# A fused adaLN transformer block on one core, its 2121 operations in another order from a new table

## The chip, the core and the metric

The kernel runs on one core of one Trainium2 chip. The core has five instruction streams that run side by side and wait for one another through semaphores: TensorE (PE, matmuls; the profile shows its weight loads apart as PEld), VectorE (DVE), ScalarE (ACT), GpSimd (POOL) and SyncE (SP, which here only issues transfers). The metric is the device time of one execution in microseconds (us); lower is better.

## The reference

The input x has 2048 rows of 640 values in bf16. A conditioning vector c gives six modulation rows, and then one transformer block is computed:

```python
mod = (silu(c) @ w_mod).reshape(1, 6, 1, -1)
sa, ca, ga, sb, cb, gb = (mod[:, i] for i in range(6))
h = layernorm(x) * (1 + ca) + sa
x = x + ga * attention(h, A_wqkv, A_wo)
h = layernorm(x) * (1 + cb) + sb
x = x + gb * (sigmoid(h @ B_w_gate) * (h @ B_w_up)) @ B_w_down
```

The attention has 32 heads of 20 values and a sliding window: row i sees the rows i - 255 to i. The hidden width of the gated part is 1536.

## The kernel before

The rows are cut into eight chunks of 256, numbered a = 0 to 7, each of two blocks of 128. For every chunk the kernel does the same steps:

- `ln1`, with `ln_stats` (L776 to L796): statistics on VectorE, the power -1/2 on GpSimd (L781, L783), the normalised block x. For the first three chunks TensorE transposes it (`pe_transposes`), and the evacuation from PSUM applies scale and shift (L858; for chunk 0 copies L839 and then modulations L846 and L847). For the other chunks SyncE transposes it by a transfer (L803) and `modulate` (L811, L812) applies scale and shift to the five parts of hT, each on VectorE, ScalarE or GpSimd.
- `qkv`: projections with wqkv (TensorE, 480 columns a matmul, 320 for chunk 0) and their evacuation (L893 on ScalarE, L894 on VectorE); Q and K are then transposed, by TensorE for chunks 0 and 1 and by SyncE's transfers for the others.
- `attention`: in two halves (q = 0, 1) of 16 heads. A half has five score groups (three for chunk 0), four of one kind and one edge group at the window's borders. All score groups write the one PSUM tile S of four banks. ScalarE takes the exponential of S into E (L1015), GpSimd zeroes what lies outside the window (L1040), and a burst of matmuls E V (L669) writes two of the four other PSUM tiles, M. The burst of one half is issued together with the second score group of the next half. `norm` on VectorE transposes, divides and transposes back (L1082, L1087, L1089, L1091), and SyncE stores the result in eight pieces in `doc` and loads it transposed as oT.
- `outproj`: output projection with wo, the first residual sum (L1164), the second layernorm, transposed by SyncE into h2T and modulated (L811, L812).
- `mlp`: twelve pairs of 128 hidden columns; matmuls with wg and wu, tanh on ScalarE (L1209), the gated product on VectorE into hh (L1211), the matmuls with wd, the second residual sum (L1230) and the store.

At the start the modulation rows are computed by matmuls of silubc (silu of c, spread) with w_mod, which lies for that time in the room of wd, wu and hh. The first two rows end as mA, needed for the first modulation. The gate rows ga and gb are spread over all partitions by a small store and a load into gbc (`gate`, `gatebc` in `mod_rows`), and multiplied into wo (L1253, five operations) and later into wd (L1192, twelve operations, VectorE or GpSimd). There is one gbc: the second load waits till the five scalings of wo have read the first. At the very start TensorE runs matmuls on zeros (L649, L660), whose result is not used.

Nothing of the order is left to the hardware or a compiler. The program makes 2121 operations in a fixed numbering, and a table `PRIO` holds one number for each. The scheduler sorts by it, and the number modulo 5 names the engine:

```python
o.prio = PRIO[self.seq] if PRIO else prio
...
for o in sorted(self.ops, key=lambda x: x.prio):
    ...
    e = ENGS[o.prio % 5]
```

ENGS is TensorE, ScalarE, VectorE, GpSimd, SyncE in that order. The walk through the sorted operations also hands out the buffers: a tile takes the slot that comes free first. Each engine's stream is then its operations in that order, with a wait on a semaphore wherever an operation depends on another engine or on a buffer's last reader (`emit`). Each engine runs its stream strictly in order, so an operation that waits holds all that stand behind it. SyncE's stream is all transfers and transposes but a few that ScalarE issues.

Of the kernel before, what the change touches and what calls it, by code (L numbers as in the profile page):

```python
# [336 lines left out]
def c_pe(n):  # L337
# [5 lines left out]
    23, 28, 258, 8, 43, 33, 958, 18, 1448, 38, 3, 507, 513, 72, 67, 48, 53, 58, 76, 84, 101, 99, 144, 149, 154, 159,  # L343
    164, 344, 169, 334, 329, 174, 584, 734, 739, 754, 604, 759, 749, 764, 594, 120, 177, 181, 192, 197, 62, 105,
    110, 115, 130, 135, 13, 125, 200, 205, 210, 215, 220, 225, 230, 345, 370, 352, 599, 2054, 1659, 1649, 729, 744,
    92, 87, 187, 237, 242, 247, 253, 263, 272, 267, 280, 275, 290, 300, 305, 286, 317, 296, 322, 311, 376, 357, 386,
    367, 362, 412, 422, 391, 417, 396, 380, 400, 406, 620, 655, 672, 515, 521, 820, 827, 465, 470, 476, 530, 535,
    541, 495, 501, 665, 677, 480, 485, 491, 565, 570, 576, 545, 551, 630, 652, 525, 555, 561, 625, 660, 681, 685,
    691, 930, 977, 765, 770, 792, 915, 920, 927, 805, 810, 816, 830, 835, 841, 437, 432, 442, 427, 447, 452, 458,
    463, 642, 647, 890, 845, 775, 900, 710, 897, 852, 797, 907, 787, 980, 985, 996, 1150, 1165, 1171, 1095, 1101,  # L350
    1375, 1382, 1195, 1250, 1257, 1262, 1210, 1296, 1385, 1392, 990, 1105, 1111, 1080, 1085, 1092, 1365, 1371, 1300,
    1351, 940, 945, 951, 971, 1155, 1161, 1190, 1231, 1215, 1220, 1226, 1280, 1285, 1292, 1330, 1337, 1344, 1619,
    1347, 1502, 2249, 1434, 2959, 1669, 1622, 1917, 1932, 2107, 2137, 1395, 1497, 1664, 2754, 1627, 1847, 339, 589,
    1022, 637, 1037, 802, 782, 912, 1043, 1048, 1053, 1058, 1237, 1485, 1410, 1455, 1435, 1305, 1492, 1421, 1462,
    1442, 1317, 1570, 1575, 1581, 1515, 1520, 1527, 1844, 1585, 1590, 1632, 1751, 1839, 1905, 1965, 2041, 2020,
    2030, 2037, 2059, 2070, 2080, 2086, 2142, 2094, 1820, 1830, 1922, 1970, 2075, 2152, 719, 724, 1007, 1002, 1017,
    1012, 937, 1027, 1033, 1063, 1068, 1203, 1242, 1209, 1249, 1453, 1548, 1536, 1543, 1471, 605, 611, 616, 695,
    706, 701, 855, 961, 881, 871, 861, 968, 888, 878, 868, 1115, 1127, 1122, 1137, 1142, 1147, 1736, 1716, 1726,
    1416, 1944, 1070, 1076, 1131, 1175, 1181, 1186, 1265, 1321, 1401, 1356, 1271, 1328, 1408, 1363, 1278, 1505,
    1597, 1512, 1602, 1612, 1772, 1896, 1891, 1886, 1881, 2049, 2310, 2315, 2322, 2155, 2160, 2327, 2205, 2210,  # L360
    2227, 2395, 2400, 2432, 2337, 2332, 2507, 2437, 2502, 2512, 2518, 2523, 2527, 2537, 2534, 2544, 2717, 2756,
    2777, 2772, 2767, 2739, 2734, 2969, 3074, 3022, 3312, 3327, 3027, 3032, 3037, 3317, 3502, 3507, 3322, 3413,
    3418, 2865, 2870, 2875, 2890, 2895, 2760, 2845, 2880, 2885, 2905, 2901, 2912, 3045, 3050, 3075, 3080, 3085,
    2915, 2920, 3055, 3060, 3065, 3091, 3097, 3110, 3115, 3170, 3175, 3180, 3100, 3105, 3185, 3195, 3200, 3191,
    3232, 3205, 3210, 3215, 3220, 3225, 3240, 3245, 3250, 3265, 3270, 3236, 3277, 3280, 3285, 3290, 3295, 3330,
    3300, 3375, 3380, 3385, 3390, 3336, 3422, 3430, 3435, 3445, 3450, 3470, 3440, 3575, 3580, 3585, 3590, 3476,
    3597, 3640, 3645, 3655, 3727, 3650, 3730, 3780, 3817, 3859, 3740, 3745, 3750, 3827, 3900, 3905, 3910, 3917,
    4476, 1700, 1705, 1862, 1710, 1800, 1902, 1914, 1690, 1695, 1746, 1782, 2189, 2390, 2405, 2412, 2145, 2300,
    2307, 2429, 2250, 2260, 2267, 2616, 2749, 1865, 1875, 1937, 1825, 1975, 1992, 1429, 1314, 1607, 1637, 1787,
    1767, 1777, 1792, 1798, 1853, 2008, 2178, 1963, 2128, 2184, 2134, 2367, 2371, 2386, 2381, 2376, 1465, 1481,  # L370
    1476, 1530, 1556, 1566, 1670, 1731, 1676, 1721, 1741, 1805, 1816, 1811, 1870, 1946, 2001, 2025, 2061, 2066,
    1553, 1763, 1758, 1563, 1688, 1683, 1928, 1858, 1953, 1958, 2013, 2018, 2095, 2101, 2231, 2202, 2217, 2222,
    2592, 2597, 2984, 2964, 2999, 2989, 3129, 2255, 2286, 2271, 2341, 2281, 2345, 2351, 2356, 2440, 2456, 2451,
    2465, 2485, 2496, 2460, 2580, 2587, 3399, 2695, 2700, 2817, 2951, 3409, 2620, 2625, 2631, 2445, 2490, 2562,
    3404, 2665, 2670, 2787, 2792, 4199, 2640, 2655, 2662, 2705, 2710, 2841, 1654, 1644, 1997, 1987, 2122, 1982,
    2112, 2117, 2168, 2173, 2193, 2243, 2603, 2608, 2424, 2744, 3346, 3261, 3306, 3041, 3011, 2565, 2576, 2571,
    2238, 2298, 2293, 2198, 2473, 2278, 2363, 2483, 2478, 2548, 2553, 2558, 2635, 2676, 2686, 2652, 2647, 2782,
    2812, 2822, 2974, 2994, 2979, 3004, 3124, 3545, 3550, 3557, 3455, 3540, 3562, 3530, 3535, 3677, 3610, 3615,
    3682, 3572, 3567, 3672, 3687, 3692, 3697, 3703, 3708, 3867, 3712, 3929, 3719, 4213, 4208, 4081, 4132, 4232,
    4220, 4280, 4285, 4290, 4325, 4215, 4310, 4315, 4320, 4335, 4331, 4357, 4345, 4350, 4370, 4375, 4380, 4340,  # L380
    4390, 4395, 4400, 4405, 4386, 4412, 4420, 4425, 4430, 4435, 4440, 4415, 4540, 4545, 4550, 4555, 4511, 4582,
    4560, 4565, 4570, 4585, 4605, 4590, 4595, 4610, 4615, 4620, 4696, 4702, 4705, 4710, 4715, 4725, 4755, 4720,
    4730, 4735, 4800, 4805, 4761, 4812, 4815, 4820, 4825, 4830, 4840, 4835, 4845, 4855, 4860, 4865, 4851, 4872,
    4900, 4905, 4910, 4917, 5215, 5220, 5225, 5382, 5389, 5175, 5180, 5185, 5192, 5360, 5365, 5400, 5407, 5934,
    2690, 2831, 2801, 2826, 2796, 2850, 2856, 2861, 2925, 3016, 3006, 3135, 3141, 3146, 2613, 2838, 2948, 2683,
    2933, 2808, 2938, 3158, 2943, 3133, 3168, 3163, 3350, 3371, 3366, 3357, 3362, 3427, 3512, 3842, 3864, 3849,
    3874, 3854, 4494, 3460, 3486, 3481, 3466, 3491, 3605, 3621, 3631, 3660, 3761, 3666, 3735, 3890, 3896, 4180,
    4185, 4247, 5034, 4105, 4115, 4122, 4177, 5164, 4110, 4160, 4167, 3885, 3970, 4047, 4174, 3995, 4000, 4006,
    4097, 5029, 3980, 3985, 3991, 4135, 4140, 4242, 2724, 2419, 3722, 2727, 3822, 3497, 3807, 3877, 3883, 3948,
    4067, 4052, 4194, 4204, 4793, 4896, 5061, 4978, 5066, 3765, 3771, 3776, 3153, 3523, 3798, 3528, 3518, 3603,  # L390
    3628, 3803, 3638, 3788, 3758, 3793, 3920, 3931, 3936, 3977, 4102, 4127, 4462, 4467, 4484, 4499, 4474, 4489,
    4649, 4920, 4930, 4987, 4925, 4940, 4992, 5015, 5020, 5077, 4935, 5050, 5082, 5002, 4997, 5007, 5092, 5087,
    5097, 5103, 5108, 5122, 5132, 5154, 5159, 5346, 5351, 5323, 5356, 5328, 5475, 5495, 5530, 5535, 5540, 5455,
    5510, 5515, 5520, 5525, 5546, 5567, 5570, 5575, 5580, 5585, 5590, 5550, 5555, 5560, 5600, 5605, 5596, 5612,
    5670, 5675, 5750, 5780, 5785, 5775, 5830, 5835, 5855, 5870, 5891, 5902, 5885, 5905, 5910, 6005, 6010, 5875,
    5880, 5915, 5920, 5925, 6016, 6022, 6050, 6055, 6060, 6065, 6070, 6025, 6030, 6035, 6040, 6045, 6076, 6082,
    6105, 6110, 6115, 6120, 6125, 6130, 6135, 6140, 6145, 6150, 6156, 6172, 6325, 6330, 6335, 6342, 6760, 6820,
    6860, 6867, 6871, 6670, 6775, 6780, 6787, 6825, 6960, 6965, 6972, 6979, 4020, 4031, 4026, 4036, 4041, 4145,
    4151, 4156, 4250, 4256, 4271, 4360, 4446, 4366, 3943, 4298, 4093, 4013, 4238, 4088, 4228, 4268, 4263, 4278,
    4308, 4303, 4450, 4531, 4526, 4517, 4502, 4522, 4627, 4632, 5044, 4659, 4654, 4639, 5059, 4600, 4661, 4686,  # L400
    4681, 4666, 4740, 4746, 4766, 4875, 4881, 4886, 6455, 6485, 6492, 6480, 6520, 6527, 6539, 6500, 6505, 6551,
    6556, 6564, 6515, 6580, 6587, 6375, 6380, 6497, 6594, 6595, 6600, 6606, 6616, 6614, 5230, 5235, 5377, 5410,
    5480, 5486, 3259, 3341, 3957, 3952, 3962, 3812, 3832, 3837, 3968, 4018, 4057, 4062, 4079, 4074, 4783, 4578,
    4772, 4507, 4692, 4960, 4971, 4966, 4458, 4673, 4678, 4538, 4788, 4778, 4753, 4958, 4798, 4948, 4893, 4953,
# [902 lines left out]
```

## Time and profile before

| | before |
|---|---|
| median of 3 runs | 325.78 us (325.57 to 326.46) |
| span of the profiled execution | 324.3 us, from the first to the last instruction |
| TensorE, matmuls | 317.3 us busy, 98% of the span |
| VectorE | 211.8 us, 65% |
| ScalarE | 212.3 us, 65% |
| GpSimd | 187.2 us, 58% |
| transfers | 37.85 MB, mean 117 GB/s |

The profiled execution has no time of its own beside its span; the time of a run is the span and what lies before and after it.

The profile gives for every instruction its start and its duration. In the order of time a row is: start, duration, engine, line of the kernel, operation, what is written from what, shape, number of instructions merged; in brackets the idle time of the engine just before, and what ended it. Matmuls are pipelined, so their durations overlap, and the cost of one in a stream is seen from start to start. In the table by stage a row is: stretch, its length, then for TensorE's matmuls, weight loads, VectorE, ScalarE and GpSimd the busy time and number of instructions; then the granted TensorE clock, the busy share of the transfer engines and the rate.

### The profile page before, as it was taken

Reading aid. Unit: us, or ns where it says so; the run is one execution under the profiler, and the core shown is the slowest. Engines: PE = TensorE matmul, PEld = TensorE weight load, DVE = VectorE, ACT = ScalarE, POOL = GpSimd, SP = SyncE. Lnnn points to the kernel's source line nnn. Section 1 sums busy time; section 2 is a strip of 40 time slices with the busy share of each in tenths; the row PEclk is TensorE's granted clock in tenths of the full one; section 3 lists DMA queues with packets and bytes.
Section 4 is the critical chain, followed back from the end, with each engine's and each line's share of the span. In section 5 each row is a group of like instructions: output and inputs, shape, how many; then the busy total and the mean of one; then the engine's idle time right before and its main releaser. Section 6 shows DMA issues by size and latency. Waiting matters only on the chain.

```text
span 324.3 us, 11594 instructions
## 1 busy us (share of the span) xinstructions
PE 317.3 (98%) x4872; PEld 222.7 (69%) x4873; DVE 211.8 (65%) x424; ACT 212.3 (65%) x316; POOL 187.2 (58%) x276
## 2 busy tenths in 40 slices
PE   8999999989999999999999999999999999999997
PEld 3564545446776568765776467877786788787885
DVE  5797898778687959674477475837463769264332
ACT  1899985889876687788687867786767764011120
POOL 5128869976668694847585939382939691012100
DMA  7998799989891383824405394340213032202101
GB/s 249 371 333 299 165 269 180 200 137 183 260 164 22 83 109 77 152 61 101 85 22 82 97 103 110 92 69 5 81 40 88 3 79 53 76 20 64 40 2 40
DMA packets 71694, 37.85 MB, mean 117 GB/s; under 512 B 45274, under 2 KB 70362, under 8 KB 71642
## 3 DMA queue, kind: packets, MB, share of 16 engines
q1 hardware_dynamic: 69616, 35.31, 48.3%
q10 hardware_dynamic: 2026, 1.80, 2.1%
q8 instruction: 38, 0.62, 0.8%
q14 instruction: 14, 0.11, 0.1%
HBM read 21.30 MB, written 5.25 MB: 82 GB/s over the span
## 4 chain that ended last, share of the span: by engine, by line
PE 73%; DMA 2%; SPq 2%; DVE 1%; POOL 1%; issue 0%; DVEq 0%
PE M L668 61%; PE S L669 6%; PE M L669 5%; DMA gbc<-gate 2%; SPq L803 2%; DVE wd L1192 1%; POOL x L793 0%; POOL st L788 0%; DVE hh L1211 0%; POOL E L1040 0%; DVE x L1230 0%; DVEq L310 0%
## 5 line engine op out<-in xcount | busy, mean ns | idle before, releaser
L1040 POOL TENSOR_SCALAR_AFFINE_SELECT E<-E 128x512 bf16<-128x512 bf16 (+1 forms) x176 | 142.6, 836 | 68.7 <-ACT E L1015 67.0
L1015 ACT ACTIVATE E<-S 128x512 bf16<-128x512 f32 (+2 forms) x184 | 150.9, 878 | 47.4 <-PE S L669 46.5
L668 PE MATMUL M<-wqkv,hT 128*128 128x480 bf16 (+1 forms) x340 | 73.9, 355 | 0.6 <-ACT hT L846 0.5
L668 PE MATMUL M<-h2T,wu 128*128 128x256 bf16 x480 | 68.0, 273 | 0.5 <-DVE hh L1211 0.5
L668 PE MATMUL M<-h2T,wg 128*128 128x256 bf16 x480 | 67.8, 273 | 0.0
L668 PE MATMUL M<-wd,hh 128*128 128x320 bf16 (+2 forms) x396 | 58.1, 295 | 0.0
L1209 ACT ACTIVATE sig<-M 128x512 f32<-128x512 f32 x48 | 28.9, 602 | 44.1 <-PE M L668 41.7
L1211 DVE SCALAR_TENSOR_TENSOR hh<-sig,M 128x512 bf16<-128x512 f32 x48 | 32.4, 681 | 37.1 <-ACT sig L1209 24.0
L668 PEld LDWEIGHTS M<-h2T,wu 128*128 128x128 bf16 x480 | 45.9, 98 | 8.4 <-issue 1.2
L668 PEld LDWEIGHTS M<-h2T,wg 128*128 128x128 bf16 x480 | 45.7, 98 | 7.1
L668 PEld LDWEIGHTS M<-wqkv,hT 128*128 128x128 bf16 x340 | 30.1, 98 | 27.6 <-DMA wqkv<-in_A_wqkv_dram 1.6
L668 PEld LDWEIGHTS M<-wd,hh 128*128 128x128 bf16 x396 | 36.8, 98 | 14.3 <-DVE hh L1211 0.2
L669 PEld LDWEIGHTS S<-QT,KT 20*64 20x64 bf16 (+1 forms) x1856 | 19.9, 100 | 21.3 <-ACT E L1015 12.0
L1230 DVE TENSOR_TENSOR x<-M,x 128x320 bf16<-128x320 f32 (+2 forms) x33 | 15.6, 476 | 27.2 <-PE M L668 27.2
L669 PE MATMUL S<-QT,KT 20*64 20x256 bf16 (+5 forms) x1856 | 32.1, 228 | 1.2 <-ACT E L1015 1.2
L776 DVE BATCH_NORM_STATS2 st<-x 128x6 f32<-128x320 bf16 x64 | 28.6, 477 | 2.3 <-DMA x<-in_A_x_dram 1.9
L1082 DVE STREAM_TRANSPOSE T<-M 128x512 f32<-128x512 f32 x32 | 21.5, 698 | 9.2 <-PE S L669 8.0
L668 PE MATMUL M<-wo,oT 128*128 128x320 bf16 x160 | 25.4, 299 | 0.0
L669 PE MATMUL M<-E,V 128*32 128x128 bf16 (+1 forms) x960 | 22.8, 246 | 0.8 <-ACT E L1015 0.4
L781 POOL TENSOR_SCALAR st<-st 128x2 f32<-128x2 f32 x16 | 3.7, 234 | 33.8 <-DVE st L778 33.6
L669 PEld LDWEIGHTS M<-E,V 128*32 128x32 bf16 x960 | 19.2, 97 | 5.3 <-issue 2.9
L1091 DVE STREAM_TRANSPOSE On<-Tn 128x1024 bf16<-128x1024 bf16 x16 | 19.8, 1240 | 0.3
(77 smaller groups left out, 240.2 us busy)
## 6 DMA issues: line engine op xcount, KB each, us to landing
x<-in_A_x_dram SPq DMA_DIRECT2D x23, 160.0 KB, 2.3
doc<-On SPq DMA_DIRECT2D x56, 40.0 KB
wd<-in_B_w_down_dram SPq DMA_DIRECT2D x4, 480.0 KB
wd<-in_w_mod_dram SPq DMA_DIRECT2D x5, 320.0 KB
wqkv<-in_A_wqkv_dram SPq DMA_DIRECT2D x4, 400.0 KB
wu<-in_w_mod_dram SPq DMA_DIRECT2D x5, 320.0 KB
oT<-doc SPq DMA_DIRECT2D x8, 192.0 KB, 2.5
out_dram<-x SPq DMA_DIRECT2D x9, 160.0 KB
```

The costliest lines, as they stand in the source:

```text
L668: return e.matmul(o, l, r, start=st, stop=sp, skip_group_check=True)
L669: return e.matmul(o, l, r, start=st, stop=sp, tile_position=tp, skip_group_check=True)
L776: A("dve", lambda e, g, bi=bi, j=j: e.bn_stats(v(bi * 12 + j * 6, 6), src[bi].ap[:, j * 320:(j + 1) * 320]), 0.48, reads=[src[bi].r()], wr ...
L781: A("pool", lambda e, g: e.tensor_scalar(v(28, n), var(), EPS, None, op0=ALU.add), 0.2, reads=[st.r(("m", bi)) for bi in range(n)], writes ...
L803: return e.dma_start_transpose(dst(), src())
L1015: A("act", lambda e, eng: e.activation(dst(), src(), ACT.Exp, scale=SM_SCALE), c_act(n), reads=[Sp.r()], writes=[E.r(key)], prio=3, tag=f" ...
L1040: A("pool", lambda e, eng: e.affine_select(rows(dst), rows(src), pattern=[[0, 8], [sign, n]], compare_op=ALU.is_ge, fill=0.0, base=base, c ...
L1082: A("dve", lambda e, g, h=h: e.transpose(T1.ap[:, 512 * h:512 * h + 512], X[h].ap), 0.694, reads=[X[h].r()], writes=[T1.r(h)], prio=3.5, t ...
L1091: A("dve", lambda e, g: e.transpose(On.ap[:], Tn.ap[:]), 1.22, reads=[Tn.r()], writes=[On.r()], prio=4, tag=f"tr2_{a}")
L1209: A("act", lambda e, g, pg=pg, sg=sg: e.activation(sg.ap[:], pg.ap[:], ACT.Tanh, scale=0.5), c_act(512), reads=[pg.r()], writes=[sg.r()], ...
L1211: A("dve", lambda e, g, pu=pu, sg=sg, f0=f0: e.scalar_tensor_tensor(out=hh.ap[:, f0:f0 + 2, :], in0=sg.ap[:].rearrange("p (a b) -> p a b", ...
L1230: A("dve", lambda e, g, ps=ps, bi=bi, c0=c0, n=n: e.tensor_tensor(x1[bi].ap[:, c0:c0 + n], ps.ap[:, 0:n], x1[bi].ap[:, c0:c0 + n], op=ALU. ...
```

## The change

Every number of `PRIO` is replaced. No operation is added, removed or altered; what changes is the place of each in its engine's stream, the engine of those that have a choice (evacuations, modulations, memory clearing, the scaling of wd, some stores and loads), and, following from the order, which buffer slot a tile takes and which waits are needed. The diff is 117 lines of numbers on each side, of which the first and the last stand here:

```diff
 PE_EPS = 0.14
 PRIO = [
-    23, 28, 258, 8, 43, 33, 958, 18, 1448, 38, 3, 507, 513, 72, 67, 48, 53, 58, 76, 84, 101, 99, 144, 149, 154, 159,
...
-    10555, 10560, 10597, 10604,
+    23, 43, 38, 63, 293, 1243, 778, 18, 773, 173, 8, 57, 13, 27, 52, 168, 68, 288, 91, 4, 106, 144, 154, 214, 234,
...
+    10585, 10590, 10597, 10604,
 ]
```

The numbers themselves say little to a reader; what follows from them is told below by comparing the streams of each engine in the two orders.

230 rows, old and new, of the table PRIO are left out of this document.

## The prediction

> **What bounds the kernel now.** I read the page's totals first, then busy time by stage, then the order of time on the stages where TensorE is not full.
>
> ```profile
> span 324.3 us, 11594 instructions
> ...
> 0.00:10.36 10.36, 8.35 (x76) 4.14 (x78) 5.92 (x20) 2.98 (x7) 4.73 (x25) 1.00 0.82 272
> 10.36:56.00 45.64, 45.10 (x625) 25.46 (x629) 39.51 (x93) 38.88 (x66) 29.09 (x45) 1.00 0.95 266
> 56.00:72.00 16.00, 14.43 (x275) 7.78 (x271) 12.35 (x24) 12.78 (x19) 14.17 (x20) 1.00 1.00 167
> 72.00:90.00 18.00, 17.49 (x288) 12.71 (x292) 13.70 (x27) 15.84 (x25) 11.29 (x15) 1.00 0.97 225
> 90.00:240.00 150.00, 149.99 (x2662) 106.55 (x2651) 97.36 (x186) 111.28 (x155) 100.12 (x135) 1.00 0.44 82
> 240.00:324.30 84.30, 81.91 (x981) 66.04 (x978) 42.95 (x79) 30.50 (x47) 27.80 (x39) 1.00 0.18 47
> ```
>
> The first pair after each stretch is its length and TensorE's busy time. What TensorE misses is 2.01 us in the first stretch, 0.54 in the second, 1.57 in the third, 0.51 in the fourth, 0.01 in the fifth and 2.39 in the last: 7.03 us in all. The kernel is one stream of matmuls, and the change alters none of them, so a new order can win only parts of these 7 us (a little more, since the ends of matmuls are modelled and a gap is at least as long as it looks) and can lose without a limit. From 90 us to the last matmul nothing is to be won. The last stretch's loss is the tail:
>
> ```profile
> 321.95 0.29 DVE x L1230
> ```
>
> This last addition and the store behind it follow the last matmul in both orders, so the tail stays. The span is 324.3 us and the median of the runs 325.78, so 1.5 us lie around the span. The sum below is made on the span.
>
> **Stage 56 to 72 us: scores wait for ScalarE.** All score groups share the one PSUM tile S, so a group can start only when the exponentials of the group before are done. First TensorE, then ScalarE (start, duration, what; in brackets the idle time before):
>
> ```profile
> 58.92 0.41 PE L669 MATMUL S<-QT,KT 20*128 20x64 bf16 x32
> 59.27 1.39 PE L668 MATMUL M<-wqkv,hT 128*128 128x480 bf16 x6
> 60.49 0.84 PE L668 MATMUL M<-wo,oT 128*128 128x320 bf16 x5
> 61.60 0.43 PE L669 MATMUL S<-QT,KT 20*64 20x256 bf16 x24 [0.27 <-ACT E L1015]
> 61.96 0.58 PE L668 MATMUL M<-wqkv,hT 128*128 128x480 bf16 x2
> 62.38 0.84 PE L668 MATMUL M<-wo,oT 128*128 128x320 bf16 x5
> 63.06 0.77 PE L668 MATMUL M<-wqkv,hT 128*128 128x480 bf16 x3
> 64.13 0.43 PE L669 MATMUL S<-QT,KT 20*64 20x256 bf16 x24 [0.30 <-ACT E L1015]
> 64.66 2.82 PE L668 MATMUL M<-wqkv,hT 128*128 128x480 bf16 x12
> 67.91 0.43 PE L669 MATMUL S<-QT,KT 20*64 20x256 bf16 x24 [0.42 <-ACT E L1015]
> 68.26 1.79 PE L668 MATMUL M<-wqkv,hT 128*128 128x480 bf16 x8
> 70.48 1.50 PE L669 MATMUL M<-E,V 128*32 128x128 bf16 x64 [0.42 <-ACT E L1015]
> ...
> 72.27 2.20 PE L668 MATMUL M<-wqkv,hT 128*128 128x480 bf16 x10
> ```
> ```profile
> 59.49 2.06 ACT L1015 ACTIVATE E<-S 128x512 bf16<-128x512 f32 x4 [0.72 <-PE S L669]
> 62.14 1.94 ACT L1015 ACTIVATE E<-S 128x512 bf16<-128x512 f32 x2 [0.59 <-PE S L669]
> 63.97 2.07 ACT L811 ACTIVATE hT<-hT,mA 128x256 bf16<-128x256 bf16 x4
> 65.93 1.92 ACT L1015 ACTIVATE E<-S 128x1536 bf16<-128x1536 f32 x2
> 68.44 1.94 ACT L1015 ACTIVATE E<-S 128x1536 bf16<-128x1536 f32 x2
> ```
>
> Prices: a projection matmul of 480 columns takes (60.49 - 59.27) / 6 = 0.203 us, an output matmul of 320 columns (63.06 - 62.38) / 5 = 0.136 us. A group of the usual kind started at 61.60, its exponentials ended at 64.08 and the next group started at 64.13: 2.53 us, of which the group itself is 0.36. So TensorE needs 2.17 us of other work between two groups. An edge group (58.92, exponentials to 61.55, next group 61.60) leaves 2.33 to fill. The order of now puts 6 projections and 5 output matmuls after the edge group (1.90 us), then 2 + 3 and 5 (1.70), then 12 (2.44), then 8 (1.62). The first two and the last are too short. The third is long enough, but four modulations (63.97 to 66.04) stand ahead of its exponentials on ScalarE. The four gaps show 0.27 + 0.30 + 0.42 + 0.42 = 1.41 of the stage's 1.57 us.
>
> **Stage 72 to 90 us: one wait.** It begins with a transfer, a gate row spread over the partitions (gbc), as the chain of waits shows; then three rows in order of time:
>
> ```profile
> 77.92 5.14 DMA gbc<-gate
> ```
> ```profile
> 83.16 2.65 DVE L1192 TENSOR_TENSOR wd<-wd,gbc 128x640 bf16<-128x640 bf16 x4 [2.12 <-DMA gbc<-gate]
> ...
> 85.72 1.27 DVE L1211 SCALAR_TENSOR_TENSOR hh<-sig,M 128x512 bf16<-128x512 f32 x2
> ...
> 86.54 1.25 PE L668 MATMUL M<-h2T,wu 128*128 128x256 bf16 x10 [0.51 <-DVE hh L1211]
> ```
>
> VectorE stood 2.12 us at the first scaling of wd, and four scalings were queued ahead of the gated products (L1211) that empty TensorE's PSUM buffers. TensorE paid 0.51 us.
>
> **The change part by part.** The table sets order and engine only. Counting operations in both orders: TensorE keeps its 907, VectorE goes from 424 to 435, ScalarE from 333 to 326, GpSimd from 264 to 260, SyncE keeps 193. The largest move is the second modulation, seven more of them on VectorE, three fewer on ScalarE and four fewer on GpSimd. TensorE changes tile shape once less (174 instead of 175 times); I cost that at nothing.
>
> *Score gaps.* The new gaps after the same edge group hold 13 output matmuls and 2 projections (13 x 0.136 + 2 x 0.203 = 2.17 us), then 13 projections (2.64), then 10 and 10 (the second with the product E V behind it). Ten last 2.20 us in the row at 72.27, and no wait follows them: just what a usual group needs. The first is short by 2.33 - 2.17 = 0.16 at most. ScalarE's modulations, now three (3 x 0.49 = 1.5 us, from the row at 63.97: four starts in 1.96), stand behind the exponentials of the group ahead of the 13: those end 2.48 after that group's start, the modulations at 3.95; the next group starts at 0.36 + 2.64 + about 0.1 for the shape change = 3.1, and its exponentials wait till 3.95 and end at 5.9. TensorE is ready again at 3.1 + 0.36 + 2.20 = 5.7, so it waits 0.2 to 0.3. Together 0.4 in place of 1.41: **-1.0 us**. Ends: all of 1.57 won; nothing won, if the transposed input of the modulations (two SyncE transposes) lands late and ScalarE stands there.
>
> *The gbc transfer.* On SyncE it now stands ahead of the last loads of wu, one K transpose and both transposes of h2T, instead of behind all but one of them. What it waits for is the scaling of wo that reads the old gbc; the last of these on VectorE has lost six statistics of 0.48 us from its front:
>
> ```profile
> L776 DVE BATCH_NORM_STATS2 st<-x 128x6 f32<-128x320 bf16 x64 | 28.6, 477 | 2.3 <-DMA x<-in_A_x_dram 1.9
> ```
>
> So gbc goes out some ten us sooner, and one scaling of wd, not four, is ahead of the first product, still one fewer than before at the third. **-0.5 us**; ends -0.6 and 0. The cover is gone if a wd load takes gbc's place as the latest (rival C).
>
> *The head.* The first projection waits for modulated input:
>
> ```profile
> 9.01 0.45 PE L668 MATMUL S<-silubc,wd 128*128 128x64 bf16 x10
> ...
> 10.36 1.92 PE L668 MATMUL M<-wqkv,hT 128*128 128x320 bf16 x12 [0.47 <-ACT hT L846]
> ```
>
> The new order takes the statistics of both first blocks before silubc's copy, and puts TensorE's transposes ahead of the last two w_mod groups. The modulation needs both these groups and the transposes; the last group (9.01) depends on a load whose landing the trace does not show apart from the queue ahead of it. Ends: 0.6 us won, if that load had long landed, 0.4 lost, if silubc's later copy holds the first group; I take **-0.1**, near nothing, because the last group still ends the chain.
>
> *Other engines and the rest.* A modulation on VectorE (lowest, median, highest ns):
>
> ```profile
> L812 DVE TENSOR_SCALAR h2T<-h2T,scB,shB x8: 327/357/840, 74.2 to 253.2; 128x256 bf16<-128x256 bf16 x8
> ```
>
> The eleven added operations cost VectorE some 11 x 0.4 us, in stages where it is busy 97 of 150 us; nothing on the path unless a product is late. Against all this stand waits that the trace of an old order cannot show. New orders of 2121 operations have them: the present one has 0.54 us between 10 and 56 us and 0.16 left over in 56 to 72. I add **+0.4**, about half of that again; ends 0 and 3 (rival C).
>
> Sum: 324.3 - 1.0 - 0.5 - 0.1 + 0.4 = 323.1 span; with 1.5 around it 324.6, or **324.5** from the median (325.78 - 1.2, rounded down because gaps are at least as long as they look).
>
> **A rule that speaks against it.** Two rows of one operation:
>
> ```profile
> 42.17 0.80 DVE L1089 TENSOR_TENSOR Tn<-T,Dr 128x640 bf16<-128x640 f32 x1
> ...
> 69.66 1.26 DVE L1089 TENSOR_TENSOR Tn<-T,Dr 128x640 bf16<-128x640 f32 x1
> ```
>
> The division took 0.80 us when GpSimd stood still and 1.26 when GpSimd ran selections. The Trainium skill, "GPSIMD Engine Reference", Key points, says that GpSimd shares its SBUF interfaces with VectorE, with contention for VectorE instructions of two SBUF inputs or in a two-port mode. The two rows agree with that. It bears on rival B.
>
> **The rivals.**
>
> *B, won and given back (no net change).* VectorE takes eleven more operations; if each meets a selection and is stretched by 1.26 - 0.80 = 0.46 us, it is 11 x (0.4 + 0.46) = 9.5 us busier, and products and evacuations come late at two or three places. At the 0.4 us of a wait as above, three such cost 1.2: 324.5 + 1.2 = 325.7. For it: gaps of exactly ten projections have no slack. Against: VectorE is idle a third of the time from 90 us on.
>
> *C, slower: the wd loads arrive last.* The load's size, and the two transposes of attention block 1 that end ahead of its stores:
>
> ```profile
> wd<-in_B_w_down_dram SPq DMA_DIRECT2D x4, 480.0 KB
> ```
> ```profile
> 70.96 1.25 DVE L1091 STREAM_TRANSPOSE On<-Tn 128x1024 bf16<-128x1024 bf16 x1
> ...
> 78.18 1.23 DVE L1091 STREAM_TRANSPOSE On<-Tn 128x1024 bf16<-128x1024 bf16 x1
> ```
>
> Now all four stand together behind the first store of attention block 1, which needs the transpose that ended at 72.2. At 4 x 0.48 MB = 1.9 MB and the 225 GB/s of the stage they last 8.5 us, to 81; at the 167 GB/s of the stage before, 11.5 us, to 84. The first scaling of wd stands on VectorE ahead of every product and right behind the second of these transposes, so it is wanted about 79.4. A hold of 2.12 us cost TensorE 0.51, so about 1.6 is free. It decides against the kernel when the hold passes some 4 us (landing after 83.5); at 5 us it costs 3.4, and 324.5 + 3.4 = 327.9. For it: the transfer share is already 0.97 and 1.00 there. Against: the first of the four is all that the first scaling needs, and a quarter of 8.5 us lands by 75.
>
> *D, the order does not do what it says* (both waits stay since ScalarE is late for other reasons): 325.8 + 0.4 = 326.2.
>
> **How the numbers follow.** Forecast 0.53, B 0.22, C 0.15, D 0.10. About 0.3%, 1 us, is what a measurement of this kernel can tell from no change: faster means below 324.8, slower above 326.76. Most of the forecast's case (0.46 of 0.53) is below 324.8, and B's lucky end adds 0.09: faster 0.55. Same: 0.07 + 0.11 + 0.05 = 0.23. Slower: C's 0.15, D's other half 0.05 and B's bad end 0.02: 0.22. The forecast's own range is 323.2 to 325.4 (all of both stages and half the head won; or one stage alone). The 8-in-10 range goes on to C's near end: 323.0 to 327.2.
>
> **What would show it.** Right: TensorE's loss between 56 and 72 us falls from 1.57 to about 0.5, no 12-projection gap follows four modulations, gbc goes out before 68 us, and VectorE has no wait for gbc or wd over 1.5 us. The first projection starts between 9.8 and 10.8. From 90 us on the loss stays under 0.3 us. Wrong: a wait of VectorE for a wd load, waits of scores for ScalarE at other places of over 1 us together, or a first projection after 11 us.

## The result and the profile after

| | before | after |
|---|---|---|
| median of 19 runs, us | 325.6 | 328.18 |
| ratio, 95% interval | | 1.0068 [1.0049, 1.0087] |
| span of the profiled run, us (its own time) | 324.3 | 328.7 (330.49) |
| granted TensorE clock of the profiled run | 1.000 | 0.995 |

The forecast was 324.5 us and faster; the kernel became slower, and by more than the range allowed. The runs of after also spread: twelve at a clock of 0.999 or 1.000 lie between 325.0 and 328.4 us (median 327.5), and six with a clock of 0.995 between 328.7 and 330.5. The nineteenth, at a clock of 1.000, took 1773.67 us; why is not known, and it does not move the median. None of 102 runs of the kernel before that stand beside the experiments shows a clock under 0.999.

First the stages of after, in the columns of the prediction's first view (length of the stretch, TensorE busy, the other engines, then granted clock, transfer share, GB/s):

```profile
0.00:10.36 10.36, 7.92 (x74) 4.00 (x76) 5.95 (x19) 1.88 (x3) 4.97 (x24) 1.00 0.84 271
10.36:56.00 45.64, 44.79 (x661) 25.97 (x656) 37.94 (x89) 39.09 (x66) 28.13 (x45) 1.00 0.94 267
56.00:72.00 16.00, 15.01 (x268) 8.05 (x249) 13.59 (x32) 12.63 (x18) 13.86 (x19) 1.00 0.82 179
72.00:90.00 18.00, 15.49 (x201) 10.29 (x201) 10.85 (x19) 11.82 (x17) 11.48 (x14) 0.91 0.55 142
90.00:240.00 150.00, 148.84 (x2609) 105.68 (x2607) 102.03 (x195) 111.39 (x156) 100.68 (x135) 1.00 0.43 87
240.00:328.70 88.70, 86.31 (x1092) 69.85 (x1089) 44.73 (x83) 33.57 (x51) 25.48 (x38) 1.00 0.19 50
```

TensorE misses 2.44, 0.85, 0.99, 2.51, 1.16 and 2.39 us: 10.34 against 7.03 before. The worst stretch, 72 to 90 us, also has a granted clock of 0.91, and matmuls at half rate count as busy there. TensorE in order of time shows both at one place:

```profile
58.23 0.41 PE L669 MATMUL S<-QT,KT 20*128 20x64 bf16 x32
58.57 1.26 PE L668 MATMUL M<-wo,oT 128*128 128x320 bf16 x8
...
61.21 2.81 PE L668 MATMUL M<-wqkv,hT 128*128 128x480 bf16 x13
63.94 0.43 PE L669 MATMUL S<-QT,KT 20*64 20x256 bf16 x24
64.30 2.33 PE L668 MATMUL M<-wqkv,hT 128*128 128x480 bf16 x10
66.75 0.43 PE L669 MATMUL S<-QT,KT 20*64 20x256 bf16 x24
67.11 2.20 PE L668 MATMUL M<-wqkv,hT 128*128 128x480 bf16 x10
69.32 1.50 PE L669 MATMUL M<-E,V 128*32 128x128 bf16 x64
70.75 0.41 PE L669 MATMUL S<-QT,KT 20*64 20x256 bf16 x20
74.51 0.22 PE L669 MATMUL S<-QT,KT 20*64 20x64 bf16 x4 [3.34 <-issue]
74.66 3.38 PE L668 MATMUL M<-wqkv,hT 128*128 128x480 bf16 x10
77.97 0.61 PE L669 MATMUL S<-QT,KT 20*128 20x64 bf16 x32
```

Down to 70.75 this is the order that the prediction counted, and no row is marked as waiting for ScalarE: the four marked waits of before are gone. Then a score group of 24 breaks off after 20 matmuls, and the other four come 3.34 us later, for "issue", that is, for nothing that a semaphore shows. One group lies within one operation, with no wait inside, which points to the instructions themselves. Behind the stop ten projections take 3.38 us where ten took 2.20: by the trace's clock record TensorE ran at half rate from 75.52 to 78.93 us. The trace has TensorE's instructions as transfers of their own (queue q8, 38 blocks of 16 KB). The seventh began at 72.01 us and had landed at 73.04, 1.47 us before TensorE went on; in the kernel before it began at 66.41.

The second new loss is at 120 us. TensorE's row, then VectorE's and GpSimd's:

```profile
120.67 0.39 PE L668 MATMUL M<-h2T,wg 128*128 128x256 bf16 x2 [0.62 <-DVE h2T L812]
121.24 1.05 PE L668 MATMUL M<-h2T,wu 128*128 128x256 bf16 x8 [0.17 <-DVE stg L894]
```
```profile
118.03 2.59 DVE L812 TENSOR_SCALAR h2T<-h2T,scB,shB 128x256 bf16<-128x256 bf16 x4
```
```profile
118.14 4.05 POOL L1040 TENSOR_SCALAR_AFFINE_SELECT E<-E 128x512 bf16<-128x512 bf16 x5 [0.60 <-ACT E L1015]
```

Four of window 1's five modulations now stand on VectorE in a row, beside GpSimd's selections: 0.65 us each, where the prediction's row had a median of 0.357. The order before had two on VectorE, two on GpSimd and one on ScalarE. Its two on VectorE took 0.74 and 0.84 us, so the stretch at this place is not new; the row of four is.

The third is the head. VectorE, then one row of GpSimd, then the first projection:

```profile
5.12 0.89 DVE L776 BATCH_NORM_STATS2 st<-x 128x6 f32<-128x320 bf16 x2 [0.97 <-DMA x<-in_A_x_dram]
...
6.18 0.43 DVE L640 COPY silubc<-siluc 128x320 bf16<-128x320 bf16 x1
7.43 1.52 DVE L796 TENSOR_SCALAR x<-x,st 128x640 bf16<-128x640 bf16 x2 [0.81 <-POOL st L783]
```
```profile
7.34 0.95 POOL L593 MEMSET Tn<- 128x1024 bf16 x1
```
```profile
11.49 0.70 PE L668 MATMUL M<-wqkv,hT 128*128 128x320 bf16 x4 [0.52 <-DVE hT L847]
```

The first projection starts at 11.49 us instead of 10.36. Two things stand out: silubc's copy behind statistics that wait for x1, and two normalisations of 1.52 us together, with a memset of GpSimd beside the first.

Last, SyncE's queue, where gbc now goes out at 62.99 us:

```profile
62.99 0.50 SPq L570 DMA_DIRECT2D gbc<-gate  x1
63.53 0.98 SPq L570 DMA_DIRECT2D wu<-in_B_w_up_dram  x2
65.77 1.57 SPq L803 DMA_TRANSPOSE KT<-stg  x1
67.45 3.98 SPq L803 DMA_TRANSPOSE h2T<-x  x2
71.52 0.47 SPq L570 DMA_DIRECT2D doc<-On  x1
72.05 2.46 SPq L570 DMA_DIRECT2D wd<-in_B_w_down_dram  x4
```

VectorE waits neither for gbc nor for wd any more. But two wu loads (1152 KB) and three transposes stand in the time in which the instruction block was wanted.

### The profile page after: what moved, and what is told of

The parts are those of the page before. It is cut to its first block, busy times and chain, and to the rows that moved or that the text cites. A ratio compares the mean times of both kernels' runs of the same rounds, so it can differ in the third digit from the quotient of the medians.

```text
span 328.7 us, 11579 instructions
## 1 busy us (share of the span) xinstructions
PE 318.4 (97%) x4872; PEld 223.8 (68%) x4873; DVE 215.1 (65%) x435; ACT 210.4 (64%) x309; POOL 184.6 (56%) x272
## 4 chain that ended last, share of the span: by engine, by line
PE 93%; DVE 3%; issue 2%; DMA 1%; POOL 0%; ACTq 0%; DVEq 0%
PE M L668 78%; PE S L669 8%; PE M L669 7%; DMA x<-in_A_x_dram 1%; DVE h2T L812 1%; DVE x L796 0%; DVE stg L894 0%; DVE hT L839 0%; POOL st L783 0%; ACTq L570 0%; DVE hT L847 0%; DVE st L776 0%; DVE V L894 0%; DVE x L1230 0%; POOL st L781 0%
## 5 line engine op out<-in xcount | busy, mean ns | idle before, releaser
L668 PE MATMUL M<-h2T,wu 128*128 128x256 bf16 x480 | 70.1, 273 | 0.2 <-DVE stg L894 0.2
L668 PE MATMUL M<-h2T,wg 128*128 128x256 bf16 x480 | 68.8, 273 | 0.6 <-DVE h2T L812 0.6
L668 PEld LDWEIGHTS M<-h2T,wu 128*128 128x128 bf16 x480 | 45.2, 98 | 8.3 <-DVE stg L894 0.5
L668 PEld LDWEIGHTS M<-wqkv,hT 128*128 128x128 bf16 x340 | 31.0, 98 | 28.1 <-issue 2.4
L894 DVE CAST stg<-M 128x480 bf16<-128x480 f32 (+1 forms) x28 | 16.4, 593 | 9.6 <-PE M L668 9.5
```

What stands on the lines that cost most here:

```text
L668: return e.matmul(o, l, r, start=st, stop=sp, skip_group_check=True)
L894: return e.tensor_copy(dst(), src())
```

## The experiments

All edits act on the table, but for E3's and a part of E13's, which change the matmuls on zeros at the start. `PRIO[x] = PRIO[y] // 50 * 50 + 5*k + e`, behind a first step that spreads the entries by ten, puts operation x right behind operation y, on engine e (1 ScalarE, 2 VectorE, 3 GpSimd, 4 SyncE). The numbers are those of the operations in the order in which the program makes them. Each run stands beside runs of the kernel before on its own chip (median 325.6 to 326.0).

**E1, the head's order.**

```diff
+PRIO[43] = PRIO[20] // 50 * 50 + 6    # cth
+PRIO[44] = PRIO[20] // 50 * 50 + 12   # siluc
+PRIO[45] = PRIO[20] // 50 * 50 + 17   # silubc, all three ahead of x1's statistics
```

> The changed kernel, with ScalarE's cth and VectorE's siluc and silubc moved ahead of the two statistics of x1, as they stood before the change. Theory (the head's loss is silubc's copy queued behind statistics that wait for x1): silubc starts near 4.9 us instead of 6.18, the first projection starts between 10.2 and 10.6 us instead of 11.49, and the median falls by 0.9 to 1.3 us, from 328.2 to about 327.1. Rival (the first projection is set by the normalised x of the second block, whose statistics now end later): the first projection stays at 11.3 to 11.6 us and the time at 328 us. The stop of TensorE near 71 to 74 us should stay in both.

silubc started at 4.49 us, the first projection at 11.64; median 327.33. The rival held as to the first projection: TensorE's transposes waited 0.93 us for the normalised x. silubc's place was not the head's loss. The median is 0.85 us lower, but the ratio to before, 1.0049 [1.0022, 1.0076], overlaps that of after, and no such gain comes from the first projection.

**E2, two modulations off VectorE.**

```diff
+PRIO[705] = PRIO[708] // 50 * 50 + 8    # to GpSimd
+PRIO[707] = PRIO[1050] // 50 * 50 + 6   # to ScalarE
```

> The changed kernel, with two of the four modulations of h2T of window 1 that VectorE has near 118 us given back: one to GpSimd right behind its own, one to ScalarE between two exponentials. Theory (VectorE's four, 0.65 us each beside GpSimd's selections, make the gate projection wait): VectorE's group of h2T ends by 119.5 us, the wait of 0.62 us before the gate matmuls (120.67 us) and the one of 0.17 us behind it are gone, the loss of TensorE in 116 to 124 us falls from 1.0 to under 0.3 us, and the median falls by 0.6 to 1.0 us to about 327.4. Rival (the gates wait for the transposes of h2T, or GpSimd's later selections hold the exponentials' masks instead): TensorE loses as much in 116 to 128 us, and the time stays at 328 us.

VectorE and TensorE of this run:

```profile
115.93 0.93 DVE L812 TENSOR_SCALAR h2T<-h2T,scB,shB 128x256 bf16<-128x256 bf16 x2
```
```profile
117.53 0.43 PE L669 MATMUL S<-QT,KT 20*64 20x256 bf16 x24
117.88 0.39 PE L668 MATMUL M<-h2T,wg 128*128 128x256 bf16 x2
118.11 1.04 PE L668 MATMUL M<-h2T,wu 128*128 128x256 bf16 x8
```

Both waits are gone, as the theory said. By start times from the first gate matmul to the last matmul of the kernel it is 243.90 us, and 245.35 in after. E3 and E4, with no such edit, have 244.95, so by these profiles 1.05 of the 1.45 is the modulations'. The median of all twelve runs stayed at 328.29, since seven of them had a clock of 0.990 to 0.995; the five at full clock have a median of 325.93, against 327.5 in after.

**E3, the same order, other instruction blocks.**

```diff
-        for k in range(2):
-            ins = e.matmul(p_S.aps[0][:, 3, :], Eall[:, 0, 0:128], Eall[:, 0, 128:640], start=True, stop=True)
+        for k in range(12):
+            ins = e.matmul(p_S.aps[0][:, 3, 0:85], Eall[:, 0, 0:128], Eall[:, 0, 128:213], start=True, stop=True)
```

> The changed kernel in exactly its order, with the ten warm-up matmuls of 512 columns at the start cut into sixty of 85 columns (the same columns and work, and their result is not used), so that every later TensorE instruction lies fifty matmuls further on in the instruction stream. Theory (the stop of 3.3 us inside a score group at 71 us is an instruction block that arrived late behind 256-byte transpose packets and the wu loads): the block that arrived at 73.04 us is now asked for about 3 us earlier, before the wu loads, so no stop over 0.5 us marked issue is seen between 66 and 80 us, the projections behind it run at a pitch of 0.20 us and not 0.40, the granted clock is 1.000, and the median falls by 2 to 4 us, from 328.2 to 324.5 to 326; the spread of its runs is under 2 us where that of the changed kernel was 5. Rival (a wait or a port conflict that belongs to the order itself): the stop stays at 71 to 75 us and the time at 328 us. A block of another place can come to lie in heavy transfers and stop TensorE there: then the stop moves, which is the theory again.

The seventh block began at 64.04 us and landed at 64.92, and the group of 24 near 72.8 us ran whole, at full clock. That is the theory's first half, and no wait of the order itself could go away by this edit. The time did not follow: median 329.01 (7 runs, two of them at 0.995). The profiled run lost 1.1 us to a late load of wqkv behind the first projection (E5 and E12 show such a wait too, of 0.44 and 0.50). With that its 327.02 us is near E4's median below (325.59 + 1.1 = 326.7), but the five runs at full clock have a median of 327.78, no better than after's 327.5. What the slower ones lost is not seen.

**E4, the two wu loads behind the transposes.**

```diff
+PRIO[220] = PRIO[383] // 50 * 50 + 9
+PRIO[222] = PRIO[383] // 50 * 50 + 14
```

> The changed kernel with the two loads of wu moved on SyncE's queue from ahead of the transposes (KT, h2T) to behind them; nothing is changed on the other engines. Theory (the instruction block is held up by the pile of wu and transposes from 63 to 73 us): the block lands before 70 us, the stop at 71 us is gone, the granted clock is 1.000 and the median falls by 2 to 4 us to 324.5 to 326; the price is a wait for wu of under 0.5 us near 81 us. Rival 1 (the transposes alone hold the block up, whatever the bulk loads do): the stop stays over 2 us. Rival 2 (nothing to do with transfers): the same stop of 3.3 us at 71 us and 328 us.

SyncE, then TensorE:

```profile
63.99 0.50 SPq L570 DMA_DIRECT2D gbc<-gate  x1
66.41 1.24 SPq L803 DMA_TRANSPOSE KT<-stg  x1
68.16 3.10 SPq L803 DMA_TRANSPOSE h2T<-x  x2
71.32 1.10 SPq L570 DMA_DIRECT2D wu<-in_B_w_up_dram  x2
```
```profile
71.39 0.43 PE L669 MATMUL S<-QT,KT 20*64 20x256 bf16 x24
71.75 2.20 PE L668 MATMUL M<-wqkv,hT 128*128 128x480 bf16 x10
73.92 0.41 PE L669 MATMUL S<-QT,KT 20*128 20x64 bf16 x32
```

Median 325.59, ratio to before 1.0005 [0.9984, 1.0025], clock 1.000 in all twelve runs; no wait for wu. One place on one queue, moved back, takes away 2.6 us, the whole loss against the kernel before. That all of it goes by the block is not shown: E3's profiled run has no stop either, and its median did not fall. The block began at 69.21 and landed at 70.15, some 1.6 us before the group that had broken off was through: the margin is small.

**E5 and E6, the memset of Tn.**

```diff
+PRIO[17] = PRIO[75] // 50 * 50 + 8    # E5, in the table after: ahead of the end of the statistics
+PRIO[17] = PRIO[77] // 50 * 50 + 8    # E6, in the table before: behind it
```

> The changed kernel, with one memset of Tn (128x1024, 0.95 us on GpSimd) moved back to where it stood before the change: ahead of the two GpSimd operations that finish the statistics of the first pair of blocks, instead of right behind them. Theory (the head's loss is VectorE's first normalisation of x stretched by this memset beside it, 1171 ns where it took 443 ns): both normalisations take 0.43 to 0.45 us, the transposes on TensorE start 0.7 us earlier, near 8.3 us, the first projection starts at 10.6 to 11.0 us instead of 11.3 to 11.6, and the runs at full clock are 0.5 to 0.8 us shorter (median near 327.0). Rival (it is the landing of x1 and the last w_mod groups that set the first projection): normalisations short, but the first projection still at 11.3 us or later.

> The kernel before the change, with only this memset of Tn moved behind the same two GpSimd operations, as the change has it. Theory: the first normalisation grows from 0.44 to about 1.17 us, the first projection goes from 10.36 to between 10.7 and 11.1 us, and the median rises by 0.4 to 0.7 us, from 325.6 to 326.0 to 326.3. Rival (the last group of w_mod, not x, sets the first projection here): no rise over 0.2 us.

The two normalisations (lowest, median, highest ns) in after, in E5 and in E6:

```profile
L796 DVE TENSOR_SCALAR x<-x,st x2: 428/800/1171, 7.4 to 8.5; 128x640 bf16<-128x640 bf16 x2
```
```profile
L796 DVE TENSOR_SCALAR x<-x,st x2: 441/444/446, 7.5 to 7.9; 128x640 bf16<-128x640 bf16 x2
```
```profile
L796 DVE TENSOR_SCALAR x<-x,st x2: 429/736/1042, 7.7 to 8.7; 128x640 bf16<-128x640 bf16 x2
```

So the memset is what stretches the first one, in either order, and the first projection goes with it: 10.93 us in E5, 11.11 in E6. Single profiles scatter here: with the memset where the change has it, seven runs with the head of after show 11.25 to 12.13 us (the last E4), with it moved back E7, E11 and E12 show 10.75, 10.86 and 11.28. The end hardly follows. In E5 TensorE then waited 0.44 us for wqkv at 11.81, and the median was 328.27 (6 runs, three of them with a low clock). In E6 it was 325.72 against 325.67, 1.0003 [0.9994, 1.0012]: E6's rival held as to the time. There the delay of 0.75 was 0.54 at the first product with V (27.94 against 27.40) and gone by 89 us: the wait at 86.54 of the order before, whose end a transfer sets, is not in E6's trace, and had taken the delay up.

**E7, E9, E10: four edits together, and two alone.** In these profiled runs a second thing varied. From the second product with V of window 0 to its last output projection the same order of matmuls takes 6.36 us in after, 6.35 in E2 and E4, but 7.86 in E1 and 7.63 in E5, since the stores of doc landed late and oT and x11 behind them on SyncE. E9 moves x11 ahead of the oT loads, E10 a transpose behind them; E7 is E2, E4, E5 and E9 in one.

```diff
+PRIO[633] = PRIO[632] // 50 * 50 + 9    # E9 and E7
+PRIO[506] = PRIO[359] // 50 * 50 + 9    # E10
```

> The changed kernel, with the load of x11 (issued at 53.86 us behind the two loads of oT, which wait for doc) moved on SyncE's queue back ahead of them, behind the load of x10. Theory (where the doc stores are late, x11 lands after VectorE wants its statistics near 57 us, and VectorE waits up to 2.3 us with the residuals behind it): no wait of VectorE for x over 0.2 us between 50 and 62 us in the profile, TensorE starts the projections behind the first out-projections without the waits of 0.4 and 0.9 us near 58 and 61 us, and the runs at full clock come closer together: median of these near 326.3 instead of 327.5, highest under 327.5. The stop near 71 us is untouched, so about a third to a half of the runs are still at 328 to 330 us with a lower clock. Rival: the spread of the runs at full clock stays at 325 to 328.4 us.

> The changed kernel with four edits together: the two wu loads behind the transposes, the load of x11 ahead of the oT loads, the memset of Tn ahead of the first statistics' end, and two of VectorE's four modulations of window 1 given to GpSimd and ScalarE. Theory: no stop marked issue over 0.5 us, clock 1.000 in all runs, first projection under 11.1 us, no wait at 119 to 121 us over 0.3 us; median 323.3 to 324.5 us, 0.3 to 0.7 per cent under the kernel before, and about 4 us under the changed kernel. Rival (the losses are not independent: a faster stretch runs into the next late transfer): 325 to 326 us.

> The changed kernel, with one transpose (KT of window 3, at 49.39 us on SyncE's queue) moved from ahead of the two loads of oT to behind them. Theory (the stores of doc share the DMA engines with this transpose and land late, oT and x11 behind them come late, and the out-projections of window 0 wait): oT is issued before 52.5 us, TensorE has no wait for oT, x or T over 0.2 us between 56 and 62 us, from the second PV group of window 0 to the last out-projection there are 6.4 us (in the profiled runs so far 6.4 to 9.8), and the runs at full clock have a median of about 326.5 instead of 327.5. The stop near 71 us and the low clock stay in a third of the runs. Rival (the doc stores are late whatever stands on SyncE): 6.4 to 8.5 us again, and no gain.

TensorE's waits between 50 and 66 us in E9, then in E10:

```profile
PE M L668 <- DMA oT<-doc: 1.9, 1, 1.9
```
```profile
PE M L668 <- DVE x L1164: 1.8, 1, 1.8
```

Neither theory held: 8.34 and 8.88 us for that stretch, medians 330.52 and 329.15 (6 runs each). With x11 forward the wait moves from x to oT. E7 came to 325.52, with three of twelve runs at a low clock, so its rival held. Its profiled run waited 1.7 us for oT, and then stopped for 1.96 us in the score group although the wu loads are behind the transposes: with oT late, the two h2T transposes ran from 69.82 to 73.28 us and the block began at 72.93. Why the doc stores land late in one execution and not in the next stays open.

**E11, three edits: E2, E4 and E5.**

> The changed kernel with three edits: wu behind the transposes, the memset of Tn ahead of the end of the first statistics, two modulations of window 1 off VectorE. Against the four edits together it leaves the load of x11 where the changed kernel has it. Theory (moving x11 forward pulled the load into the doc stores' time and made oT later): the median is 323.3 to 324.5 us, with clock 1.000 in at least ten of twelve runs, from 325.6 with wu alone by 0.4 to 0.7 for the memset and 1.1 for the modulations. Rival (the late oT is there with or without x11): about 325 us with some runs over 327.

Median 324.50, ratio 0.9957 [0.9942, 0.9973], clock 1.000 in all nine runs. Its stages, the third to the fifth:

```profile
56.00:72.00 16.00, 15.84 (x304) 8.79 (x296) 13.48 (x32) 12.63 (x18) 14.19 (x20) 1.00 0.78 135
72.00:90.00 18.00, 18.00 (x308) 13.09 (x305) 13.86 (x27) 13.70 (x21) 13.01 (x16) 1.00 0.90 249
90.00:240.00 150.00, 150.00 (x2622) 106.90 (x2619) 100.77 (x193) 113.14 (x157) 101.62 (x138) 1.00 0.42 83
```

From 56 to 240 us TensorE misses 0.16 us, against 2.09 before. Between 10.36 and 56 us it misses 2.11, against 0.54: the largest part is a wait of 1.12 us for ScalarE's exponentials at 52.52. This version is faster than both kernels.

**E12 and E13, E11 with the transpose of E10, and that with the warm-up in 35 pieces of 146 columns.**

> The three edits and the KT transpose of window 3 behind the loads of oT. Theory: the sum of the parts without the late oT: median 322.8 to 323.8 us, spread of the runs under 2 us, 0.5 to 0.9 per cent under the kernel before. Rival (the moved transpose meets the instruction block or the next transposes): 324.5 us or more, with a stop in the profile elsewhere.

> As the run before, with the ten warm-up matmuls of 512 columns cut into thirty-five of 146, so that every later TensorE instruction lies twenty-five further on in the stream. Theory (an instruction block that is asked for while the KT and h2T transposes run, 66 to 72 us, has to wait for them; asked for earlier it comes at once): the block that came at 72.0 us in the changed kernel begins to arrive between 63.5 and 65.5 us, no wait marked issue over 0.3 us at 66 to 80 us, clock 1.000 in all runs, median equal to the run before within 0.4 us or lower. Rival: the block still comes after 68 us.

Medians 325.61 and 325.75: the transpose's move gains nothing here either. In E13 the seventh block began at 65.48 us (the edge of what was expected) and no "issue" was seen between 66 and 80, in E12 at 70.83 with none over 0.3; the median did not gain by it. The clock fell all the same in two runs of E12 and one of E13. E13's is the profiled one, and there the half rate has nothing to do with the block: the filler of 35 pieces was done early, TensorE waited 1.99 us for silubc, and the half rate ran from 7.80 to 11.21 us.

**E14 and E15, wu ahead in the old order, and half of E4.**

```diff
+PRIO[222] = PRIO[220] // 50 * 50 + 9    # E14, in the table before
+PRIO[222] = PRIO[383] // 50 * 50 + 9    # E15, in the table after
```

> The kernel before the change, with its second load of wu moved on SyncE's queue up behind the first, so that both stand ahead of the transposes of hT, QT and h2T, as the change has them; nothing else. Theory (two wu loads ahead of the transposes make the instruction block of that time late): the block that begins at 66.4 us in the kernel before begins after 68 us, in part of the runs TensorE stops in a score group near 72 us and the clock is below 1.000, and the median rises by 0.5 to 3 us to between 326.3 and 329. Rival (the loads are not the cause; the new order of TensorE itself brings the block's request and its need too near together): block at 66 to 67 us, clock 1.000 in all runs, and 325.7 to 326.0 us.

> The changed kernel, with only one of its two wu loads moved behind the transposes. Theory (the longer the bulk ahead of the transposes, the later the block): the block begins between 69.2 us (both moved) and 72.0 us (none moved), a low clock in fewer than a third of the runs, median between 325.6 and 327.5. Rival (moving any load off this place is enough or nothing is): the same as with both moved, 325.6 us, or as with none, 328.2 us.

E14: block at 68.94 us instead of 66.41, but no stop, clock 1.000 in all runs, 325.94 us, 1.0018 [1.0003, 1.0032]. E15: block at 68.40, a stop of 0.69 us, one of twelve runs at 0.995, median 326.16. So E14's theory held as to the block and its rival as to the time: two wu loads ahead of the transposes make the block 2.5 us later even in the old order, which still has it in time. The new order, short of waits, wants it sooner: by the records TensorE breaks off behind its 976th matmul in after, which starts at 70.98 us, and starts its 977th at 72.64 in E14. For the time it takes both, the loads and the new order; E7 shows that late transposes can hold the block without the loads. That the block is the later the more is loaded was not borne out step by step: one load moved gave 68.40, both 69.21.

All profiled runs at this place together, from the trace:

| run | block begins, lands | TensorE goes on | stop, us | runs with clock under 0.999 |
|---|---|---|---|---|
| before | 66.41, 67.54 | | none | 0 of 102 |
| E6 | 66.86, 67.93 | | none | 0 of 11 |
| E14 | 68.94, 70.01 | | none | 0 of 12 |
| after | 72.01, 73.04 | 74.51 | 3.34 | 6 of 19 |
| E1 | 71.77, 72.86 | 74.28 | 0.97 | 3 of 12 |
| E2 | 68.92, 71.41 | 72.77 | 1.80 | 7 of 12 |
| E5 | 70.89, 71.92 | 73.47 | 0.96 | 3 of 6 |
| E9 | 74.02, 75.05 | 76.65 | 3.34 | 3 of 6 |
| E10 | 72.84, 73.95 | 75.38 | 1.78 | 2 of 6 |
| E7 | 72.93, 74.40 | 75.83 | 1.96 | 3 of 12 |
| E15 | 68.40, 69.51 | 71.67 | 0.69 | 1 of 12 |
| E4 | 69.21, 70.15 | | none | 0 of 12 |
| E11 | 69.31, 70.24 | | none | 0 of 9 |
| E12 | 70.83, 71.78 | | none | 2 of 12 |
| E3 | 64.04, 64.92 | | none | 2 of 7 |
| E13 | 65.48, 66.36 | | none | 1 of 12 |

All eight runs that stopped broke off at the same place, behind the 20th matmul of the same group. They went on 1.36 to 1.60 us after the landing (2.16 in E15). With both wu loads ahead of the transposes 24 of 61 runs have a low clock (after, E1, E2, E5, E9, E10; E3, whose stream is shifted, adds 2 of 7), with both behind 6 of 57 (E4, E7, E11 to E13). The last column counts half rate anywhere in a run: in E13 it stands at the start, and in E7 one of two stretches is behind the wait for oT.

## Why the prediction was wrong

*Score gaps, -1.0.* Right, and too small. E4, whose order of matmuls is that of after, loses 0.17 us between 56 and 72 us instead of 1.57: -1.4. The 0.2 to 0.3 us that ScalarE's three modulations were to cost did come, but no row marks them. In after the ten projections from 64.30 to the group at 66.75 take 2.45 us, the next ten, from 67.11 to 69.32, take 2.21, and the group at 66.75 starts just behind these exponentials of ScalarE:

```profile
64.68 1.93 ACT L1015 ACTIVATE E<-S 128x512 bf16<-128x512 f32 x2
```

The old order's waits were larger than marked in the same way: its twelve projections from 64.66 to the group at 67.91 took 3.25 us, some 0.6 more than twelve need (2.20 for ten, 0.41 for two), and 0.42 was marked.

*The gbc transfer, -0.5.* Right. It went out at 62.99 us, VectorE had no wait for gbc or wd, and E4 loses nothing between 72 and 90 us, against 0.51 before. Rival C's mechanism, wd landing last, is refuted, though its sign was the right one.

*The head, -0.1, ends 0.6 won and 0.4 lost.* The first projection came 1.13 us later, outside both ends. The step looked at VectorE's and TensorE's order alone. E1 shows that silubc's place was not it; E5 and E6 show the memset on GpSimd, which the prediction never named among the moved work, by 0.56 and 0.75 us of the first projection. The rest of the 1.13 is not told apart. In time the term was worth little: E6 finds no rise.

*Other engines, "nothing on the path unless a product is late".* Four modulations in a row were late. This is rival B, at one place in place of two or three, and dearer: 1.0 us.

*New waits, +0.4, ends 0 and 3 (held to rival C).* This is the step that failed. It set one number, from the leftovers of the old order, for waits with no name. One had a name that was not thought of: the transfer of TensorE's own instructions, with a price of its own (3.34 us of stop, then about 1.1 us for ten projections at half rate) in part of the runs. The paragraph on gbc had listed what it passed on SyncE, wu and three transposes, and asked only what gbc gained by it, not what else moves with these transfers. E4 puts the place of the two wu loads at 2.6 us of the median; how much of that is the stop and the half rate, and how much came about in another way, stays open (E3).

From 328.18 the wu loads take 2.6 (E4, 325.59), and the modulations and the memset 1.1 more (E11, 324.50): the forecast's own figure, 324.5. That they meet to the tenth is luck: the score gaps gave 1.4 for 1.0, and E11 has a wait that neither the sum nor the order before has. But what was forecast to be won in the two stages was won, and what was not foreseen cost 3.7 us.

## What to carry to other kernels

Before bulk loads are moved together on a queue, look up when the next instruction block of the busiest engine is due: here a stop marked "issue" in the middle of one operation's instructions went with a late block, and a filler that shifts the stream took it away. Such a filler can disturb its own place, as E13's did. When a table moves work, read every engine's rows beside the path, the memsets too, and ask at what price the operation beside them runs. Take medians and clocks of many executions: the single profiled run of E3 looked cured, and its median was not.

## What the runs showed of the hardware

TensorE's instruction blocks take 0.88 to 2.49 us in the sixteen profiled runs, 1.03 in the middle, and where transposes are under way the other transfers can nearly stand still for a part of that time and behind it. In after, around the landing at 73.04 (the window 72.9 to 74.1 us in 40 slices, the wd loads at its end):

```profile
GB/s 0 0 0 0 9 0 9 9 9 9 9 9 9 17 9 9 9 9 9 9 9 17 9 9 9 9 9 9 17 9 9 9 17 119 273 282 282 379 290 444
```

A stop of well under 3 us was followed by half the clock: 1.80 us in E2, with the row behind it,

```profile
72.77 0.22 PE L669 MATMUL S<-QT,KT 20*64 20x64 bf16 x4 [1.80 <-issue]
72.93 3.65 PE L668 MATMUL M<-wqkv,hT 128*128 128x480 bf16 x10
```

and 1.78 and 1.96 in E10 and E7, while 0.96 and 0.97 (E5, E1) were not. Of two waits for oT, 1.7 us in E7 was followed by it and 1.9 in E9 was not. By the clock records each stretch of half rate between the first and the last matmul lasts 3.41 us, so a run's clock of 0.994 or 0.995 stands for one of them and 0.990 for two; the two in E7 begin at 59.79 and 76.86 us, five times 3.41 apart. The Trainium skill, "TensorE: Matmul & The Clock Gate", Part 1, puts the fall behind at least one idle window of about 3.4 us, and has the windows run freely. The length and E7's spacing agree with that; a window idle throughout does not. Even in after the 3.41 us ahead of the fall (72.11 to 75.52) have TensorE at work again from 74.51, and in E2, E10 and E7 the stop fills little more than half of them. What decides is open.

The memset stretched a normalisation from 0.44 to 1.17 us, 0.73 for a neighbour of 0.95. The Trainium skill, "GPSIMD Engine Reference", Key points, has GpSimd share its SBUF interfaces with VectorE, with contention for VectorE instructions in a two-port mode or of two SBUF inputs. The stretch agrees with that sharing; whether this normalisation, which has one SBUF tensor as input beside its statistics, ran in such a mode no run here shows.
